# A three-stage kernel whose second products go out two steps at a time at every second step, while the weights are being decoded

## The chip, the core and the metric

The kernel runs on one core of a Trainium2 chip. The metric is the device time of one execution in microseconds (us), the median of several runs. TensorE is called PE here, VectorE DVE, ScalarE ACT, GpSimd POOL, SyncE SP, as in the profile.

## What is computed

A causal convolution over 4 sequences of 4096 tokens with 192 channels, 7 taps and one softmaxed set of taps for each of 8 heads, and then two layers of the form "product, function, product" on the 16384 tokens:

```python
out = np.einsum('hk,bskhg->bshg', w, x_unf)   # w: softmax over the 7 taps
h = x @ w_in                                  # 192 -> 2048
g = h * np.cos(h)
x = g @ w_out                                 # 2048 -> 192
h = x @ w_in2
g = np.where(h > 0.0, h, 1.0 * (np.exp(np.minimum(h, 0.0)) - 1.0))
return g @ w_out2
```

The four weight matrices come as 64-bit floats. The kernel turns each into a pair of 32-bit tiles, a high and a low part, from its two 32-bit words. That is what "decoding" means below.

## The kernel before, in words

**Tiles and steps.** The tokens are 32 blocks of 512. The 2048 hidden channels of a block are done in 8 steps of two tiles of 128. So a step is (layer m, block b, pair j), and there are 512 steps in a list made at lines 509 to 516: four blocks of layer 1, the same four of layer 2, the next four of layer 1, and so on. The first two blocks of layer 1 are each split into two runs of four steps.

**First products (A).** `products_A` makes one hidden tile `u` from x: 9 products of 64 rows each. The two tiles of a step, t = 2s and 2s + 1, use the two halves of PE's rows and stand side by side, 18 products in 9 slots (`side_by_side`, line 577). Each `u` takes the next of four PSUM banks in a ring (lines 518 to 523), so the tiles of step s reuse the banks of step s - 2.

**Elementwise work.** For a tile of layer 1, ACT makes `w` from `u` (line 608, `emit_act1`), DVE subtracts (line 617, `emit_mid`), ACT takes the sine (line 623, `emit_act2`), DVE multiplies by `u` (line 631, `emit_g`; the last reader of the bank), ACT rounds to `gh` (line 637, `emit_hi`), POOL makes `gl` = w - gh (line 644, `emit_lo`). `gh` and `gl` have six buffers each, three steps' worth. Layer 2 has no line 617, and line 633 in the place of line 631.

**Second products (B).** `LAG` = 3 steps later, `gh` and `gl` of a step go into the accumulators. In blocks that begin while weights are still being decoded this is `whole_B`: 10 products over all 128 rows (line 567), placed behind the first products. Two accumulator banks do for it, since the other two PSUM banks hold the decoding's tiles `t`. Once decoding is over (`late`), blocks use `products_B`, 20 products of 64 rows that stand side by side with the first products.

**Order.** The schedule is written out by hand, by the order in which `step` (line 874) emits. It emits all products of step s first, and then for i = 0, 1 and t = 2s + i:

```python
if now:
    emit_act1(t)
    emit_mid(t)
...
if 0 <= t - 1 < 2 * total:
    emit_act2(t - 1)
    emit_g(t - 1)
...
if 0 <= t - 2 < 2 * total:
    emit_hi(t - 2)
    emit_lo(t - 2)
```

Between these stand pieces of the decoding (`advance`: lines 195 to 207 on ACT, DVE and POOL, one piece in most steps, at i = 1), the convolution of later blocks (line 376 on DVE), and the reading out of finished accumulators (`evac`: lines 659, 666, 697). Each engine works its own instructions off in order. The steps with `whole_B` are 0 to 31, layer 1 of the first four blocks; their second products are emitted in steps 3 to 34.

Of the kernel before, what the change touches and what calls it, by code (L numbers as in the profile page):

```python
# [23 lines left out]
LAG = 3  # L24
# [8 lines left out]
def conv_then_two_mlps(ctx, tc, x, weight, w_in1, w_out1, w_in2, w_out2, out):  # L33
# [275 lines left out]
    late = []  # L309
# [3 lines left out]
    def bank(tag, name):  # L313
        pool = ps_u if tag[0] == "u" else ps_a if tag[0] == "a" else late[0]
        return pool.tile([P, N], F32, tag=tag, name=name)
# [181 lines left out]
    def double_z(b):  # L497

        zh, zl, zc = zs.pop(b)
        doubled.add(b)  # L500
        sh, sl, ch, cl = doubles()
        swap(sh, zh)
        swap(sl, zl)
        both_halves(ch, zc[half[0]])
        both_halves(cl, zc[half[1]])
        xs[2, b] = {"oh": zh, "ol": zl, "sh": sh, "sl": sl, "ch": ch, "cl": cl}
        yield

    steps, b0 = [], 0
# [15 lines left out]
    acc, hid, wrk, gs = {}, {}, {}, {}  # L525

    def products_A(t):

        (m, b, j), i = steps[t // 2], t % 2
        x, p = xs[m, b], half[i]  # L530
        u = hid[t] = ring_bank("u")
        ops = [(k, w, h) for k in ("cos" if t > 1 else "ocs") for w, h in (("h", "h"), ("l", "h"), ("h", "l"))]
        for n, (k, w, h) in enumerate(ops):
            at = wi[m, w, "c"][p, j] if k == "c" else wi[m, w, "o"][p, j, i if k == "o" else 1 - i]
            yield u, at, x[k + h][p], n == 0, n == len(ops) - 1

    def products_B(s, i):

        m, b, j = steps[s]
        if (m, b) not in acc:  # L540
            acc[m, b] = [bank(k, "acc") for k in ("a0", "b0", "a1", "b1")]
        o, c, p = acc[m, b][i], acc[m, b][2 + i], half[i]
        h, l, sel = (wo[m, n] for n in ("h", "l", "s"))
        ops = []
        for f in (2 * j, 2 * j + 1):
            gh, gl = gs[f"{s} {f % 2}"]
            st, sp = f == 0, f == NF - 1
            for to, w, g, first, final in ((o, l, gh, st, False), (o, h, gh, False, False), (c, sel, gh, st, False), (o, h, gl, False, sp), (c, sel, gl, False, sp)):
                ops.append((to, w[p, f], g[p], first, final))
        if s == total - 1:  # L550
            ops = [ops[n] for n in (2, 4, 7, 0, 1, 9, 3, 5, 6, 8)]
        yield from ops

    def whole_B(s):

        m, b, j = steps[s]
        begins, stops = (j % (NP // 2) for j in (j, j + 1)) if split_up(m, b) else (j, (j + 1) % NP)
        if not begins:
            acc[m, b] = [bank(k, "acc") for k in ("a0", "a1")]
        o, c = acc[m, b]  # L560
        h, l, sel = (wo[m, n] for n in ("h", "l", "s"))
        (gh0, gl0), (gh1, gl1) = gs[f"{s} 0"], gs[f"{s} 1"]
        f0, f1 = 2 * j, 2 * j + 1
        st, sp = not begins, not stops
        ops = [(o, l, f0, gh0), (o, h, f0, gh0), (c, sel, f0, gh0), (o, l, f1, gh1), (o, h, f1, gh1), (c, sel, f1, gh1), (o, h, f0, gl0), (c, sel, f0, gl0), (o, h, f1, gl1), (c, sel, f1, gl1)]
        for n, (to, w, f, g) in enumerate(ops):
            nc.tensor.matmul(to, lhsT=w[:, f], rhs=g, start=st and n in (0, 2), stop=sp and n >= len(ops) - 2)  # L567

    whole = set()

    def split_up(m, b):
        return m == 1 and b < 2

    def ends_here(m, b, j):
        return j == NP - 1 or split_up(m, b) and j == NP // 2 - 1

    def side_by_side(*streams):

        for pr in zip_longest(*streams):
            for product in pr:  # L580
                if product:
                    o, lhsT, rhs, first, final = product
                    nc.tensor.matmul(o, lhsT=lhsT, rhs=rhs, start=first, stop=final)  # L583

    def products(s):
        now, then = 0 <= s < total, 0 <= s - LAG < total
        if then and steps[s - LAG][2] == 0 and not late:
            whole.add(steps[s - LAG][:2])
        if not then or steps[s - LAG][:2] in whole:
            if now:  # L590
                side_by_side(products_A(2 * s), products_A(2 * s + 1))
            if then:
                whole_B(s - LAG)
        elif not now:
            side_by_side(products_B(s - LAG, 0), products_B(s - LAG, 1))
        else:
            streams = products_B(s - LAG, 0), products_B(s - LAG, 1)
            side_by_side(chain(products_A(2 * s), streams[0]), chain(streams[1], products_A(2 * s + 1)))
        if then:
            for i in (0, 1):  # L600
                del gs[f"{s - LAG} {i}"]

    def emit_act1(s):
        m = steps[s // 2][0]
        u = hid[s]
        w = wk.tile([P, N], F32, tag="w", name="w", bufs=5)
        if m == 1:
            nc.scalar.activation(out=w.bitcast(I32), in_=u, func=AF.Copy, bias=0.25)  # L608
        else:
            nc.scalar.activation(out=w, in_=u, func=AF.Relu, scale=-1.0)  # L610
        wrk[s] = w

    def emit_mid(s):
        m = steps[s // 2][0]
        u, w = hid[s], wrk[s]
        if m == 1:
            nc.vector.scalar_tensor_tensor(out=w, in0=u, scalar=0.25, in1=w.bitcast(I32), op0=ALU.add, op1=ALU.subtract)  # L617

    def emit_act2(s):
        m = steps[s // 2][0]  # L620
        w = wrk[s]
        if m == 1:
            nc.scalar.activation(out=w, in_=w, func=AF.Sin, scale=6.283185)  # L623
        else:
            nc.scalar.activation(out=w, in_=w, func=AF.Exp, scale=-1.0)  # L625
# [9 lines left out]
    def emit_hi(t):  # L635
        gh = wk.tile([P, N], F32R, tag="gh", name="gh", bufs=6)
        nc.scalar.activation(out=gh, in_=wrk[t], func=AF.Copy)  # L637
        gs[f"{t // 2} {t % 2}"] = [gh]
# [8 lines left out]
    def evac(m, b, j):  # L647

        if split_up(m, b):
            return first_part(m, b) if j < NP - 1 else second_part(m, b)  # L650
        if (m, b) in whole:
            return whole_evac(m, b)
        return half_evac(m, b)
# [184 lines left out]
    def need(m, at, *kinds):  # L838
        while any(ready.get((k, m), 0) < at for k in kinds):
            assert loaded or any(stages.values())  # L840
            advance()
# [13 lines left out]
    def begin_split(b):  # L855
        while b not in conved:
            next(cq, None)
        for _ in split(b):
            yield
# [14 lines left out]
    def step(s):  # L874
        now = 0 <= s < total
        present[0] = s
        if now:
            m, b, j = steps[s]
            need(m, j + 1, "o", "c")
        finish = iter(())  # L880
        if 0 <= s - LAG < total:
            m, b, j = steps[s - LAG]
            need(m, 2 * j + 2, "oh", "os")
        products(s)
        ends = 0 <= s - LAG < total and ends_here(*steps[s - LAG])
        if ends:
            assert not lazy
            finish = evac(*steps[s - LAG])
        if s in begin_at:
            m, b = begin_at[s]  # L890
            chores.append(begin_split(b) if m == 1 else double_z(b))
        first_mlp = now and steps[s][0] == 1
        for i in (0, 1):
            t = 2 * s + i
            if i:
                next(finish, None)
# [3 lines that stand above are left out]
            next(finish, None)  # L900
# [3 lines that stand above are left out]
            if not prepared and (s < NP // 2 or i != ends and (s < 12 or not ends and (s % 3 or s > 18))):  # L904
                advance()
# [3 lines that stand above are left out]
            if i:  # L909
                next(finish, None)  # L910
            if now and not first_mlp and not ends:
                next(cq, None)
                if i and not first_mlp and steps[s][2] in (4, 6):
                    next(cq, None)
            chore()
        if prepared and not late:
            brief.close()
            top.close()
            late.append(ctx.enter_context(tc.tile_pool(name="ps_s", bufs=1, space=bass.MemoryType.PSUM)))

    total = len(steps)
# [119 lines left out]
```

## Time and profile before

| | |
|---|---|
| Median of 3 runs | 2296.68 us (2296.4 to 2298.99) |
| Profiled execution: its own time / its span | 2297.01 / 2295.3 us |
| PE, DVE, ACT, POOL busy, share of the span | 99%, 77%, 81%, 55% |
| Chain that ended last: PE / DVE | 89% / 8% |
| Granted TensorE clock, mean | 0.997 |
| Line 567, products of the whole form | 47 to 222 us, 32 steps |

All stages bar the first tenth look alike: PE has no gap, and two kinds of product share its rows. The change concerns the stretch from 45 to 222 us alone, so the page's shares of the whole span say little about it. It is read from the order in time of PE's products in that stretch, from what ended the gaps between them, and from what DVE and ACT did meanwhile. A row of the order in time gives the start in us, the duration in us, the engine, the line and the operation, and in a bracket the idle time ahead of it and what ended that.

### The profile page before, as it was taken

Reading aid. Unit: us, or ns where it says so; the run is one execution under the profiler, and the core shown is the slowest. Engines: PE = TensorE matmul, PEld = TensorE weight load, DVE = VectorE, ACT = ScalarE, POOL = GpSimd, SP = SyncE. Lnnn points to the kernel's source line nnn. Section 1 sums busy time; section 2 is a strip of 40 time slices with the busy share of each in tenths; the row PEclk is TensorE's granted clock in tenths of the full one; section 3 lists DMA queues with packets and bytes.
Section 4 is the critical chain, followed back from the end, with each engine's and each line's share of the span. In section 5 each row is a group of like instructions: output and inputs, shape, how many; then the busy total and the mean of one; then the engine's idle time right before and its main releaser. Section 6 shows DMA issues by size and latency. Waiting matters only on the chain.

```text
span 2295.3 us, 49382 instructions
## 1 busy us (share of the span) xinstructions
PE 2265.7 (99%) x19226; PEld 1839.5 (80%) x19226; DVE 1768.8 (77%) x2564; ACT 1862.8 (81%) x3422; POOL 1253.0 (55%) x975
## 2 busy tenths in 40 slices
PE   8999999999999999999999999999999999999998
PEld 5667888888888888888888888888888888888887
DVE  7986977779777897778967798676986779777655
ACT  6877788888888788888788888888788887888886
POOL 5895335763367533674446743576435763367532
PEclk9999999999999999999999999999999999999999
DMA  7222221213211132112221123212221113211111
GB/s 167 81 68 49 51 58 36 46 32 64 49 36 38 32 69 48 40 29 57 52 52 33 24 58 55 47 38 44 45 57 35 46 34 64 42 36 38 26 38 22
DMA packets 292603, 111.43 MB, mean 49 GB/s; under 512 B 245840, under 2 KB 260176, under 8 KB 292368
## 3 DMA queue, kind: packets, MB, share of 16 engines
q1 hardware_dynamic: 290048, 107.42, 22.4%
q8 instruction: 150, 2.46, 0.4%
q10 hardware_dynamic: 2320, 0.85, 0.2%
q14 instruction: 85, 0.70, 0.1%
HBM read 30.09 MB, written 12.58 MB: 19 GB/s over the span
## 4 chain that ended last, share of the span: by engine, by line
PE 89%; DVE 8%; issue 1%; ACT 1%; DMA 1%; POOL 0%; ACTq 0%; DVEq 0%; SPq 0%; POOLq 0%
PE acc L583 45%; PE u L583 42%; DVE y L376 1%; PE acc L567 1%; DVE w L633 1%; DVE w L631 1%; DVE w L617 1%; DVE gl L644 1%; DVE t L202 1%; DVE w L203 0%; DMA raw<-in_moe_w_in_dram 0%; DMA raw<-in_moe_w_out_dram 0%; DVE y L374 0%; DVE raw L199 0%; PE y L403 0%
## 5 line engine op out<-in xcount | busy, mean ns | idle before, releaser
L644 POOL TENSOR_TENSOR gl<-w,gh 128x512 fp32r<-128x512 f32 x768 | 1013.7, 1321 | 1001.8 <-ACT gh L637 640.0
L583 PE MATMUL acc<-gh,wo_hl 64*128 64x512 f32 x3840 | 1174.3, 386 | 0.0
L583 PEld LDWEIGHTS acc<-gh,wo_hl 64*128 64x128 f32 x3840 | 705.3, 184 | 75.8 <-DVE z L697 0.4
L583 PE MATMUL acc<-gh,wo_s 64*128 64x512 f32 x1920 | 740.8, 386 | 0.0
L583 PE MATMUL acc<-gl,wo_hl 64*128 64x512 f32 x1920 | 740.2, 386 | 0.0
L583 PE MATMUL acc<-gl,wo_s 64*128 64x512 f32 x1920 | 740.1, 386 | 0.0
L637 ACT ACTIVATE gh<-w 128x512 fp32r<-128x512 f32 x1024 | 641.2, 626 | 16.2 <-DVE w L633 15.8
L583 PE MATMUL u<-ch,wi_c 64*128 64x512 f32 x2048 | 619.4, 391 | 14.1 <-DVE w L631 11.4
L583 PE MATMUL u<-sh,wi_o 64*128 64x512 f32 x2048 | 611.4, 387 | 0.0
L617 DVE SCALAR_TENSOR_TENSOR w<-u,w 128x512 f32<-128x512 f32 x512 | 352.0, 687 | 251.1 <-ACT w L608 249.1
L633 DVE SCALAR_TENSOR_TENSOR w<-w,u 128x512 f32<-128x512 f32 x512 | 347.8, 679 | 215.1 <-ACT w L625 210.0
L610 ACT ACTIVATE w<-u 128x512 f32<-128x512 f32 x512 | 306.2, 598 | 186.7 <-PE u L583 167.1
L608 ACT ACTIVATE w<-u 128x512 int32<-128x512 f32 x512 | 306.4, 598 | 184.2 <-PE u L583 178.5
L583 PE MATMUL u<-z,wi_o 64*128 64x512 f32 x1536 | 427.4, 386 | 0.0
L583 PEld LDWEIGHTS u<-ch,wi_c 64*128 64x128 f32 x2048 | 364.7, 184 | 71.7 <-DVE w L631 18.9
L583 PEld LDWEIGHTS u<-sh,wi_o 64*128 64x128 f32 x2048 | 368.5, 185 | 40.7
L583 PE MATMUL u<-sl,wi_o 64*128 64x512 f32 x1024 | 387.1, 387 | 0.0
L583 PE MATMUL u<-cl,wi_c 64*128 64x512 f32 x1024 | 386.7, 387 | 0.0
L583 PEld LDWEIGHTS acc<-gh,wo_s 64*128 64x128 f32 x1920 | 353.3, 184 | 37.9 <-DVE e L698 0.3
L583 PEld LDWEIGHTS acc<-gl,wo_hl 64*128 64x128 f32 x1920 | 353.3, 184 | 37.6
L583 PEld LDWEIGHTS acc<-gl,wo_s 64*128 64x128 f32 x1920 | 353.2, 184 | 37.6
L631 DVE TENSOR_TENSOR w<-u,w 128x512 f32<-128x512 f32 x512 | 348.8, 681 | 41.4 <-ACT w L623 41.4
(143 smaller groups left out, 3608.2 us busy)
## 6 DMA issues: line engine op xcount, KB each, us to landing
out_dram<-e SPq DMA_DIRECT2D x189, 64.0 KB, 2.0
xa<-in_x_dram SPq DMA_DIRECT2D x124, 88.0 KB, 2.9
sh<-z SPq DMA_DIRECT2D x64, 128.0 KB, 2.9
sl<-z SPq DMA_DIRECT2D x64, 128.0 KB, 2.5
ch<-z SPq DMA_DIRECT2D x64, 128.0 KB, 2.4
cl<-z SPq DMA_DIRECT2D x64, 128.0 KB, 2.4
sh<-xh SPq DMA_DIRECT2D x62, 128.0 KB, 2.3
sl<-xl SPq DMA_DIRECT2D x62, 128.0 KB, 2.3
```

The source lines that it names most:

```text
L202: nc.vector.tensor_scalar(out=t, in0=size, scalar1=2.0 ** -15, scalar2=2.0 ** 17 - 2.0 ** 13, op0=ALU.max, op1=ALU.min)
L376: nc.vector.scalar_tensor_tensor(out=o, in0=i, scalar=w, in1=o, op0=ALU.mult, op1=ALU.add)
L567: nc.tensor.matmul(to, lhsT=w[:, f], rhs=g, start=st and n in (0, 2), stop=sp and n >= len(ops) - 2)
L583: nc.tensor.matmul(o, lhsT=lhsT, rhs=rhs, start=first, stop=final)
L608: nc.scalar.activation(out=w.bitcast(I32), in_=u, func=AF.Copy, bias=0.25)
L610: nc.scalar.activation(out=w, in_=u, func=AF.Relu, scale=-1.0)
L617: nc.vector.scalar_tensor_tensor(out=w, in0=u, scalar=0.25, in1=w.bitcast(I32), op0=ALU.add, op1=ALU.subtract)
L631: nc.vector.tensor_tensor(out=w, in0=u, in1=w, op=ALU.mult)
L633: nc.vector.scalar_tensor_tensor(out=w, in0=w, scalar=-1.0, in1=u, op0=ALU.add, op1=ALU.max)
L637: nc.scalar.activation(out=gh, in_=wrk[t], func=AF.Copy)
L644: eng.tensor_tensor(out=gl, in0=wrk.pop(t), in1=f32(own[0]), op=ALU.subtract)
```

## The change

At even steps the second products of the two steps s - 4 and s - 3 are emitted together, behind the first products of step s. At odd steps there are none. This holds for blocks in the whole form; blocks of the other form are as before. Nothing is computed differently, and no buffer is added.

```diff
-    def products(s):
-        now, then = 0 <= s < total, 0 <= s - LAG < total
-        if then and steps[s - LAG][2] == 0 and not late:
-            whole.add(steps[s - LAG][:2])
-        if not then or steps[s - LAG][:2] in whole:
+    def is_whole(s):
+        if steps[s][2] == 0 and not late:
+            whole.add(steps[s][:2])
+        return steps[s][:2] in whole
+
+    def due(s):
+        if not 0 <= s - LAG < total:
+            return []
+        if not is_whole(s - LAG):
+            return [s - LAG]
+        return [s - LAG - 1, s - LAG] if (s - LAG) % 2 else []
+
+    def products(s, then):
+        now = 0 <= s < total
+        if not then or is_whole(then[0]):
             if now:
                 side_by_side(products_A(2 * s), products_A(2 * s + 1))
-            if then:
-                whole_B(s - LAG)
+            for k in then:
+                whole_B(k)
...
-        if 0 <= s - LAG < total:
-            m, b, j = steps[s - LAG]
+        then = due(s)
+        for k in then:
+            m, b, j = steps[k]
             need(m, 2 * j + 2, "oh", "os")
-        products(s)
-        ends = 0 <= s - LAG < total and ends_here(*steps[s - LAG])
+        products(s, then)
+        ends = bool(then) and ends_here(*steps[s - LAG])
```

The order on PE, before, around one step of the whole form: from the last first products of one step to the start of the next step's. `u` is a hidden tile, `acc` an accumulator; 128x512 is the output.

```order
L583 MATMUL u<-sl,wi_o 128x512 x2
L567 MATMUL acc<-gh,wo_hl 128x512 [waits Pool_49]
L567 MATMUL acc<-gh,wo_hl 128x512 [waits Activation_49]
L567 MATMUL acc<-gh,wo_s 128x512
L567 MATMUL acc<-gh,wo_hl 128x512 x2
L567 MATMUL acc<-gh,wo_s 128x512
L567 MATMUL acc<-gl,wo_hl 128x512
L567 MATMUL acc<-gl,wo_s 128x512
L567 MATMUL acc<-gl,wo_hl 128x512
L567 MATMUL acc<-gl,wo_s 128x512
L583 MATMUL u<-ch,wi_c 128x512 [waits DVE_49] x2
```

On PE after the change, from the last first products of an odd step, through all first products of the even step behind it, to the first second product:

```order
L583 MATMUL u<-sl,wi_o 128x512 x2
L583 MATMUL u<-ch,wi_c 128x512 [waits DVE_49] x2
L583 MATMUL u<-ch,wi_c 128x512 x2
L583 MATMUL u<-cl,wi_c 128x512 x2
L583 MATMUL u<-xh,wi_o 128x512 x4
L583 MATMUL u<-xl,wi_o 128x512 x2
L583 MATMUL u<-sh,wi_o 128x512 x4
L583 MATMUL u<-sl,wi_o 128x512 x2
L567 MATMUL acc<-gh,wo_hl 128x512 [waits Pool_49]
```

What moved: the ten second products that stood between two steps' first products are gone from behind the odd step, and stand as a second ten behind the even step's.

On DVE the order is the same before and after. This is the change's, with the tiles' numbers (u_834 and u_835 are step 8's, u_907 and u_908 step 9's, u_956 step 10's; lines 628 and 642 are lines 617 and 631 of before):

```order
L628 SCALAR_TENSOR_TENSOR w_927<-u_907,w_927 128x512 [waits Activation_49]
L642 TENSOR_TENSOR w_885<-u_835,w_885 128x512 [waits Activation_49]
L628 SCALAR_TENSOR_TENSOR w_936<-u_908,w_936 128x512 [waits Activation_49]
L642 TENSOR_TENSOR w_927<-u_907,w_927 128x512 [waits Activation_49]
L199 SCALAR_TENSOR_TENSOR raw_173<-raw_173,t_95 128x512 [waits DMAHW7_49,DMAHW0_49]
L202 TENSOR_SCALAR t_95<-w_897 128x512 [waits DVE_49]
L203 TENSOR_SCALAR w_897<-t_95 128x512 [waits DVE_49]
```

Nothing moved here: the last reading of step 8's second bank (u_835) stands behind the first instruction that needs step 9's first products (u_907). What moved is PE's side of it.

On ACT the order of the work is the same too, and a wait is another. Before, in step 8:

```order
L637 ACTIVATE gh_881<-w_815 128x512 [waits DVE_49]
L608 ACTIVATE w_885<-u_847 128x512 [waits PE_49,Pool_49]
L623 ACTIVATE w_876<-w_876 128x512 [waits DVE_49]
L254 ACTIVATE wo1_hl_475<-w_709 128x512 [waits Pool_49]
L195 ACTIVATE t_95<-raw_173 128x512 [waits DMAHW7_49,DMAHW0_49]
```

After:

```order
L648 ACTIVATE gh_881<-w_803 128x512 [waits DVE_49,PE_49]
L619 ACTIVATE w_885<-u_835 128x512 [waits Pool_49]
L634 ACTIVATE w_876<-w_876 128x512 [waits DVE_49]
L254 ACTIVATE wo1_hl_475<-w_699 128x512 [waits Pool_49]
L195 ACTIVATE t_95<-raw_173 128x512 [waits DMAHW7_49,DMAHW0_49]
```

What moved is the wait on PE, from the reading of `u` to the writing of `gh`: that buffer's last reader now stands on PE behind the same step's first products. POOL's and SP's instructions stand as before.

## Rows read from the trace of the kernel before

**Rows 1.** The chain that ended last, from the page: shares of the span.
```profile
PE 89%; DVE 8%; issue 1%; ACT 1%; DMA 1%; POOL 0%; ACTq 0%; DVEq 0%; SPq 0%; POOLq 0%
```

**Rows 2.** Busy time by stretch (PE, PEld, DVE, ACT, POOL), then clock, DMA share, GB/s.
```profile
44.90:221.50 176.60, 164.31 (x897) 114.30 (x896) 146.94 (x214) 139.88 (x260) 141.63 (x109) 0.98 0.32 80
221.50:398.10 176.60, 176.60 (x1555) 145.46 (x1556) 141.53 (x202) 144.89 (x267) 74.39 (x56) 1.00 0.23 46
```

**Rows 3.** Order in time on PE, one step without gaps: start, duration, instruction.
```profile
192.79 0.73 PE L583 MATMUL u<-ch,wi_c 64*128 64x512 f32 x4
...
194.74 0.39 PE L583 MATMUL u<-sl,wi_o 64*128 64x512 f32 x2
195.06 0.73 PE L567 MATMUL acc<-gh,wo_hl 128*128 128x512 f32 x2
...
195.86 0.62 PE L567 MATMUL acc<-gh,wo_hl 128*128 128x512 f32 x2
...
197.25 0.40 PE L567 MATMUL acc<-gl,wo_s 128*128 128x512 f32 x1
197.58 0.50 PE L583 MATMUL u<-ch,wi_c 64*128 64x512 f32 x2
```

**Rows 4.** Order in time on ACT and DVE behind those first products.
```profile
195.22 0.60 ACT L608 ACTIVATE w<-u 128x512 int32<-128x512 f32 x1 [1.32 <-PE u L583]
195.72 0.62 ACT L623 ACTIVATE w<-w 128x512 f32<-128x512 f32 x1
...
196.46 0.68 DVE L631 TENSOR_TENSOR w<-u,w 128x512 f32<-128x512 f32 x1
```

**Rows 5.** DVE's last reading of a bank, and the product on PE that waited for it.
```profile
101.70 0.68 DVE L631 TENSOR_TENSOR w<-u,w 128x512 f32<-128x512 f32 x1
...
102.44 0.74 PE L583 MATMUL u<-ch,wi_c 64*128 64x512 f32 x3 [0.56 <-DVE w L631]
```

**Rows 6.** PE's waits from 44 to 222 us: total, times, longest.
```profile
PE u L583 <- DVE w L631: 11.4, 13, 1.8
```

**Rows 7.** Order in time on PE: four long waits, and the next step's start behind two.
```profile
56.75 0.73 PE L583 MATMUL u<-ch,wi_c 64*128 64x512 f32 x3 [1.77 <-DVE w L631]
...
63.07 0.73 PE L583 MATMUL u<-ch,wi_c 64*128 64x512 f32 x4
...
114.12 0.73 PE L583 MATMUL u<-ch,wi_c 64*128 64x512 f32 x3 [1.62 <-DVE w L631]
...
136.10 0.80 PE L583 MATMUL u<-ch,wi_c 64*128 64x512 f32 x3 [1.52 <-DVE w L631]
...
142.44 0.73 PE L583 MATMUL u<-ch,wi_c 64*128 64x512 f32 x4
...
160.80 0.73 PE L583 MATMUL u<-ch,wi_c 64*128 64x512 f32 x3 [1.69 <-DVE w L631]
```

**Rows 8.** PE by stretch behind three of these waits; the last-but-two column is the clock.
```profile
57.90:61.20 3.30, 3.30 (x15) 0.53 0.44 110
...
115.90:119.20 3.30, 3.15 (x17) 1.00 0.86 152
...
136.40:139.70 3.30, 3.30 (x17) 0.53 0.02 5
```

**Rows 9.** Order in time on DVE: first line 617 of steps 3, 5, 7, 9, 17, 19.
```profile
48.04 0.69 DVE L617 SCALAR_TENSOR_TENSOR w<-u,w 128x512 f32<-128x512 f32 x1 [3.57 <-ACT w L608]
...
60.14 0.69 DVE L617 SCALAR_TENSOR_TENSOR w<-u,w 128x512 f32<-128x512 f32 x1 [0.19 <-ACT w L608]
...
72.16 0.68 DVE L617 SCALAR_TENSOR_TENSOR w<-u,w 128x512 f32<-128x512 f32 x1
...
84.28 0.68 DVE L617 SCALAR_TENSOR_TENSOR w<-u,w 128x512 f32<-128x512 f32 x1
...
127.77 0.68 DVE L617 SCALAR_TENSOR_TENSOR w<-u,w 128x512 f32<-128x512 f32 x1
...
140.20 0.69 DVE L617 SCALAR_TENSOR_TENSOR w<-u,w 128x512 f32<-128x512 f32 x1
```

More of the change, by code (lines that the diff above doesn't have):

```diff
@@ L583, in side_by_side @@
                     nc.tensor.matmul(o, lhsT=lhsT, rhs=rhs, start=first, stop=final)
-    def products(s):
-        now, then = 0 <= s < total, 0 <= s - LAG < total
-        if then and steps[s - LAG][2] == 0 and not late:
-            whole.add(steps[s - LAG][:2])
-        if not then or steps[s - LAG][:2] in whole:
+    def is_whole(s):
[11 more added lines that the diff above has]
+        if not then or is_whole(then[0]):
             if now:
                 side_by_side(products_A(2 * s), products_A(2 * s + 1))
-            if then:
-                whole_B(s - LAG)
+            for k in then:
+                whole_B(k)
         elif not now:
-            side_by_side(products_B(s - LAG, 0), products_B(s - LAG, 1))
+            side_by_side(products_B(then[0], 0), products_B(then[0], 1))
         else:
-            streams = products_B(s - LAG, 0), products_B(s - LAG, 1)
+            streams = products_B(then[0], 0), products_B(then[0], 1)
             side_by_side(chain(products_A(2 * s), streams[0]), chain(streams[1], products_A(2 * s + 1)))
-        if then:
+        for k in then:
             for i in (0, 1):
-                del gs[f"{s - LAG} {i}"]
+                del gs[f"{k} {i}"]
     def emit_act1(s):
@@ L880, in step @@
         finish = iter(())
-        if 0 <= s - LAG < total:
-            m, b, j = steps[s - LAG]
+        then = due(s)
+        for k in then:
+            m, b, j = steps[k]
             need(m, 2 * j + 2, "oh", "os")
-        products(s)
-        ends = 0 <= s - LAG < total and ends_here(*steps[s - LAG])
+        products(s, then)
+        ends = bool(then) and ends_here(*steps[s - LAG])
         if ends:
```

## The prediction, made before the changed kernel was run

> **What bounds the kernel now.** I read the chain of the page first: PE is 89% of it, one line of products after another [rows 1]. So time is won or lost where PE is held up, or where its own products get cheaper. Then I split the busy times by stretch. In the 176.6 us from the first product of step 3 to that of step 35, the stretch that the change touches, PE works 164.3 us; in the next 176.6 us it works all of them [rows 2]. So PE has 12.3 us of gaps in the changed stretch and none behind it, and whatever that stretch gains or loses is handed on whole to the end. In the changed stretch DVE is at 147 of 176.6 us [rows 2], so it is near to being a second limit.
>
> Then the order in time on PE, in a step without a gap [rows 3]. It takes 197.58 - 192.79 = 4.79 us: 2.27 us from the first A product to the first B product, 2.52 us from there to the next step's A. Within B six products go out in 197.25 - 195.86 = 1.39 us, so a slot is 0.232 us. The step has 9 + 10 = 19 slots, 4.40 us. The other 0.39 us lie at the two changes between A (two products of 64 rows side by side) and B (128 rows).
>
> Then who waits for whom. Of the 12.3 us of gaps 11.4 us are one kind of wait, 13 times: a first product waits for DVE's last reading of its bank [rows 6]. So the ring of four banks is what couples PE to DVE, and the change alters just what stands between two users of a bank.
>
> **What is saved.** With two B together, each pair of steps has one change from A to B and one back, where it had two of each. There are 16 pairs, so 16 x 0.39 = 6.2 us less on PE [rows 3].
>
> **What is added.** The two tiles of step s reuse the banks of step s - 2. The last reading of the second of them is the line 631 of tile 2(s - 2) + 1. On DVE it stands behind the line 617 of step s - 1's first tile, on ACT its sine stands behind that tile's line 608, and both of these need step s - 1's A to be complete. So from the end of one step's A to the second product of the next step's A there is always a chain through ACT and DVE. Its length, from a step in which neither engine had a backlog: A's last products start at 194.74 and take 0.39, so they end at 195.13 [rows 3]; line 608 starts at 195.22, line 623 at 195.72, line 631 at 196.46 for 0.68, so it ends at 197.14 [rows 4]. That is 2.01 us. From there to the released product it is 0.06 us: 101.70 + 0.68 = 102.38, against 102.44 [rows 5].
>
> Before, B's 2.52 us lie over this chain, so it shows only where DVE is late. After the change nothing lies between an odd step's A and the even step's A. The cover is gone there, 16 times, and it is useless where two B follow one another: behind the even step's A PE has 2 x 10 slots to do.
>
> So a pair costs PE, where nothing else is late: A of the even step to B 2.27, ten slots and the change back 2.52, another ten slots 2.32, the odd step's A 2.34 to its end (192.79 to 195.13), the chain 2.01 and 0.06. Sum 11.52 us, against 2 x 4.79 = 9.58 us. The sum over the stretch: step 3's A and its chain 2.34 + 2.07 = 4.41; fifteen pairs at 11.52 = 172.8; the last even step with its two B 2.27 + 2.52 + 2.32 = 7.11. That is 184.3 us, against 176.6 us [rows 2]: **+7.7 us**. The 6.2 us saved are in it, and so are the old waits, which go, as DVE now has 11.52 us for what it did in 11.0 on average.
>
> **Where DVE is slower than that.** Some pairs have more than 11.52 us of DVE work. From the first line 617 of one odd step to that of the next it was: steps 3 and 4 60.14 - 48.04 = 12.10, less the idle 0.19 in the second row's bracket, 11.91; 5 and 6 12.02; 7 and 8 12.12; 17 and 18 12.43 [rows 9]. The excess over 11.52 is 0.4 + 0.5 + 0.6 + 0.9 = 2.4 us at most, as DVE may still have been idle for some tenths inside the others; I take **+2.0 us**. I found no other pair with more than 11.52 us of work.
>
> **What the clock adds.** Four old waits are about as long as the new one. Behind 56.75 and 136.10 the granted clock fell to the lower of its two levels, 1.2 GHz (0.53 on average over 3.3 us, so 0.5 for nearly all of it); behind 114.12 it stayed at 1.00 [rows 7, 8], and so it did behind 160.80. The two falls cost 63.07 - 56.75 = 6.32 and 142.44 - 136.10 = 6.34 us for a step that takes 4.79 [rows 3, 7], so 1.54 us each. The new wait, shown as such a row shows it (behind the lone first product, which starts one slot after A's last and takes 0.50), would be idle for about 2.46 - 0.23 - 0.50 = 1.73 us. The nearest rows are 1.77, which fell, and 1.69, which did not; 1.62 did not and 1.52 did [rows 7]. The bounds are none and all 16. I take 10: a little over the half that the four show, since 1.73 is at the long end of them. That is 10 x 1.54 = 15.4 us, less what the pairs limited by DVE absorb, 2.0 x 10/16 = 1.3: **+14.1 us**.
>
> The Trainium skill (TensorE: Matmul & The Clock Gate, section Why this matters for your kernels) warns only of idle gaps longer than any wait here. By that the clock would not fall at all, and the sum would be 2306.4. The trace disagrees: it fell behind idle times of 1.77 and 1.52 us [rows 7, 8].
>
> **What I cost at nothing.** `gh` of an even step's first tile now waits for the third product of the first B. In the step of the rows that product would start a slot before 195.86, at 195.63, and be out some 0.4 us later, at 196.03; ACT first does lines 608 and 623, until 195.72 + 0.62 = 196.34 [rows 3, 4]. Its second `gh` and POOL's `gl` wait for products that are out before their engines get there. The cover is the two B, 4.8 us in which ACT and POOL have only that step to do; if it failed, 0.3 us a pair, 5 us in all, would be the price. The decoding is placed by step and not by time, so DVE, ACT, POOL and SP do the same in the same order, DMAs too. Reading out a finished accumulator gets a step more of room; the 0.9 us of PE's gaps that are not line 631's [rows 2, 6] go, inside the sum above.
>
> **The sum.** 2297.0 us (the profiled execution) + 7.7 + 2.0 + 14.1 = 2320.8. The median of the runs is 0.3 us lower, so 2320.5 us.
>
> **Rivals.**
> 1. *The wait comes, the clock hardly falls.* 2297.0 + 9.7 - 0.3 = 2306.4 us with no fall, 1.5 us more for each of a few. For it: two of the four long waits left the clock alone. Against it: sixteen waits of one length come one behind the other, and some must lie as those that fell.
> 2. *Faster.* The new wait takes the place of the old ones, which are there already for 11.4 us [rows 6], and the saved changes remain: 2296.7 - 6.2 = 2290.5 us. This decides at one point: the last reading of the second bank would have to end within a slot of the odd step's last A product. For it: where DVE has a backlog, it has the next tile's input before PE asks. Against it: by the order on DVE that reading stands behind an instruction that needs those very products, so 2.0 us are the least, and where DVE has no backlog it takes 2.01 us [rows 3, 4].
> 3. *No difference.* The saved changes and the freed backlog of DVE pay for the new wait, about 2297 us. This needs the chain at 1.5 us instead of 2.07; no row shows it so short.
> 4. *Slower still.* All waits pull the clock down, and `gh` costs its 0.3 us a pair: 2297.0 + 9.7 + 16 x 1.54 - 2.0 + 5 = 2334 us.
> That the change doesn't do what it says is excluded: PE's order shows 16 pairs.
>
> **Chances.** The forecast, with five to fourteen falls: 0.58. Rival 1: 0.25. Rival 2: 0.08. Rival 3: 0.04. Rival 4: 0.05. Differences under 0.2% (4.6 us) are about what a measurement of this kernel can't tell from none. So faster 0.08, same 0.04, slower 0.88. The range: rival 1 without any fall, and 2 us for the error of a chain taken from one step (16 x 0.13), give 2304; fourteen falls, 14 x 1.54 = 21.6, less 1 that DVE's pairs absorb, plus the same 2, give 2329. Rivals 2 to 4 are left out, 0.17 in all.
>
> **What would show it.** In the changed kernel, line 567's products in groups of twenty; 16 waits of a first product for DVE's line of `g`, each 1.5 to 1.8 us as the rows count, some 27 us in all in the place of 11.4; a granted clock of about 0.9 instead of 0.98 in the stretch, with 0.5 for 3 us behind many of the waits; the first split products at 240 to 248 us instead of 221.5; and everything behind that as before, only later. The prediction is wrong if those waits are few or short, if the clock stays at 1.00, or if the time comes from behind 250 us.

## The result, and the profile after

| | before | after |
|---|---|---|
| Median | 2297.3 us | 2323.8 us |
| Lowest to highest | 2296.4 to 2298.99 | 2323.12 to 2327.97 |
| Profiled execution: time / span | 2297.01 / 2295.3 us | 2323.89 / 2322.2 us |
| Mean granted clock | 0.997 | 0.990 |

The ratio is 1.0118, with a 95% interval of 1.0101 to 1.0136. The kernel became slower by 26.5 us, where 23.8 us were forecast.

The busy times by stretch of the kernel after, columns as in [rows 2]. The first line runs from the first product of step 3 to that of step 35, the same pieces of work as the first of [rows 2]:

```profile
45.50:248.80 203.30, 170.31 (x899) 124.31 (x898) 151.04 (x216) 141.80 (x262) 140.24 (x109) 0.91 0.28 69
248.80:425.40 176.60, 176.60 (x1559) 145.95 (x1560) 141.46 (x200) 144.44 (x266) 73.95 (x55) 1.00 0.24 46
```

The stretch takes 203.3 us where it took 176.6. That is 26.7 us, the whole loss; behind it PE works all the time again, as before. PE's gaps went from 12.3 to 33.0 us, and its busy time from 164.3 to 170.3 us though it has the same products to do: the clock is 0.91 instead of 0.98.

PE's waits in the stretch, total, times and longest, are the counterpart of [rows 6] (line 642 is line 631 of before, line 644 its like in layer 2):

```profile
PE u L583 <- DVE w L642: 31.2, 15, 3.5
PE u L583 <- DVE w L644: 1.8, 1, 1.8
```

There are sixteen of them, one for each pair, and together they are all of PE's 33.0 us of gaps. The order in time on PE, one pair in which the clock stayed up and the start of the next:

```profile
204.30 0.73 PE L583 MATMUL u<-ch,wi_c 64*128 64x512 f32 x3 [1.95 <-DVE w L642]
...
211.35 0.73 PE L583 MATMUL u<-ch,wi_c 64*128 64x512 f32 x4
...
213.31 0.40 PE L583 MATMUL u<-sl,wi_o 64*128 64x512 f32 x2
213.54 0.39 PE L583 MATMUL u<-ch,wi_c 64*128 64x512 f32 x1
215.77 0.77 PE L583 MATMUL u<-ch,wi_c 64*128 64x512 f32 x3 [1.83 <-DVE w L642]
...
228.74 0.73 PE L583 MATMUL u<-ch,wi_c 64*128 64x512 f32 x3 [1.83 <-DVE w L642]
```

And what ACT and DVE did between 213.31 and 215.77:

```profile
213.79 0.60 ACT L619 ACTIVATE w<-u 128x512 int32<-128x512 f32 x1 [3.53 <-PE u L583]
214.29 0.62 ACT L634 ACTIVATE w<-w 128x512 f32<-128x512 f32 x1
...
215.03 0.68 DVE L642 TENSOR_TENSOR w<-u,w 128x512 f32<-128x512 f32 x1
```

The odd step's A ends at 213.31 + 0.40 = 213.71. DVE's last reading ends at 215.71, 2.00 us later, and the released product starts at 215.77. From one such release to the next it is 215.77 - 204.30 = 11.47 us here, and 228.74 - 215.77 = 12.97 us in the next pair. The difference is the clock, by stretch (PE busy, clock, DMA share, GB/s):

```profile
216.30:219.70 3.40, 3.40 (x16) 0.50 0.00 0
...
204.40:207.70 3.30, 3.30 (x22) 1.00 0.02 5
```

Behind the release at 204.30 PE started 22 products in 3.3 us; behind the one at 215.77 it started 16 in 3.4 us, at 1.2 instead of 2.4 GHz. Ten of the sixteen waits are followed by such a fall, nine times of about 3.4 us and once, behind 138.93, of 6.8.

### The profile page after: what moved, and what is told of

Read it like the earlier page. It is cut to its first block, busy times and chain, and to the rows that moved or that the text cites. A ratio compares the mean times of both kernels' runs of the same rounds, so it can differ in the third digit from the quotient of the medians.

```text
span 2322.2 us, 49396 instructions
## 1 busy us (share of the span) xinstructions
PE 2270.5 (98%) x19226; PEld 1862.8 (80%) x19226; DVE 1772.8 (76%) x2564; ACT 1862.6 (80%) x3422; POOL 1250.5 (54%) x975
## 4 chain that ended last, share of the span: by engine, by line
PE 91%; DVE 6%; issue 1%; ACT 1%; DMA 0%; ACTq 0%; POOL 0%; DVEq 0%; POOLq 0%
PE acc L583 45%; PE u L583 43%; PE acc L567 3%; DVE y L376 1%; DVE w L644 1%; DVE gl L655 1%; DVE w L642 1%; DVE w L628 1%; DVE t L202 0%; DVE y L374 0%; ACT w L619 0%; DMA raw<-in_moe_w_in_dram 0%; PE y L403 0%; DVE raw L199 0%; DVE w L203 0%
```

## The experiments

Theory: the new wait is the chain from the odd step's A through ACT and DVE to the last reading of the second bank; it is 2 us long, comes 16 times, and the clock falls behind most of them. Rivals: twenty second products in a row cost something by themselves, for instance through `gh` and `gl`, which come free later; only the clock counts, or does not count at all; the loss belongs to the decoding.

**The chain taken away.** In the changed kernel, at the start of odd steps, the instructions of the tile before go first:

```diff
+            early = i == 0 and 3 <= s < 34 and s % 2 == 1
+            if early:
+                emit_act2(t - 1)
+                emit_g(t - 1)
             if now:
                 emit_act1(t)
                 emit_mid(t)
             next(finish, None)
-            if 0 <= t - 1 < 2 * total:
+            if not early and 0 <= t - 1 < 2 * total:
                 emit_act2(t - 1)
                 emit_g(t - 1)
```

> The change, with the sine and the product by u of the tile before (lines 623 and 631 of before) emitted ahead of lines 608 and 617 at the start of each odd step from 3 to 33. My theory (the new wait is the chain from the odd step's first products through ACT and DVE to the last reading of the second bank): that reading no longer needs the odd step's products, the 16 waits go, the clock stays up, and the 16 x 0.39 us of saved changes remain where DVE is not the limit: 2290 to 2297 us. Rival (twenty second products in a row cost by themselves, through gh and gl that come free later): about 2315 to 2324, as the changed kernel. Rival (only the clock counts): waits stay at 1.8 us, 2305 to 2324.

Measured: 2301.33 us against 2298.96 us before, ratio 1.0009 (0.9999 to 1.0018). Some 24 of the 26.5 us are gone, with the second products still in twenties. That speaks for the chain and against the rivals that put the cost on the twenties themselves. The size expected was not met: the time should have come out under before. PE's waits of this run, and two starts of odd steps' A in a part without any wait:

```profile
PE u L583 <- DVE w L642: 18.2, 14, 2.5
...
197.19 0.73 PE L583 MATMUL u<-ch,wi_c 64*128 64x512 f32 x4
...
206.30 0.73 PE L583 MATMUL u<-ch,wi_c 64*128 64x512 f32 x4
```

Where nothing waits, a pair takes 206.30 - 197.19 = 9.11 us, where it took 9.58 before [rows 3]. So the saving on PE is real, 0.47 us a pair. But 18.2 us of other waits are left, more than the 11.4 us of before, and the clock of the stretch is 0.95, from five falls. One of these waits on DVE, ending with line 642 at 141.53:

```profile
138.92 1.27 DVE L677 SCALAR_TENSOR_TENSOR rows<-acc,rows 128x512 f32<-128x512 f32 x2
140.12 0.73 DVE L376 SCALAR_TENSOR_TENSOR y<-xT,wch,y 128x512 f32<-128x512 f32 x1
141.53 0.69 DVE L642 TENSOR_TENSOR w<-u,w 128x512 f32<-128x512 f32 x1 [0.68 <-ACT w L634]
```

The reading out of an accumulator (line 677) and a convolution tap (line 376) stand ahead of the reading that PE waits for, and ACT's sine for it stands behind a reading that needs line 677. With two A in a row PE asks for that bank right away; with ten B in between it asked 2.5 us later [rows 3]. The other thirteen waits were not followed up in this way.

**The control.** The same reordering in the kernel before, without the change.

> The same reordering in the kernel before, as a control. My theory: before, the second products lie over the chain, and the 11.4 us of waits there come from DVE's work for the decoding; putting one 0.6 us instruction later changes little: 2292 to 2298 us. If the reordering is worth more than 5 us by itself, what the run before this one gains is not the change's.

Measured: 2297.15 us against 2298.96 us, ratio 0.9997 (0.9988 to 1.0006). No difference, as expected. So what the reordering won in the changed kernel it won by taking the new wait away, and not by something of its own.

**The wait kept, PE kept busy.** In the changed kernel, eight copies of a first product in front of the even step's A:

```diff
+                a, c = products_A(2 * s), products_A(2 * s + 1)
+                if then:
+                    head = next(a)
+                    for _ in range(8):
+                        nc.tensor.matmul(head[0], lhsT=head[1], rhs=head[2], start=True, stop=True)
+                    a = chain([head], a)
-                side_by_side(products_A(2 * s), products_A(2 * s + 1))
+                side_by_side(a, c)
```

> The change, with eight copies of the even step's first product (64 rows, into the same free bank, overwritten by the real one) in front of it, so that PE works for about 1.85 of the 2.0 us of the wait. The result is the same. My theory of the clock (it falls behind these waits, 11 times in the trace, for 1.5 us each): the waits' place in time stays, no fall, 2323.8 - 11 x 1.5 = 2307 us (2304 to 2311). Rival (the falls cost nothing, since DVE or ACT set the pace): 2320 or more.

Measured: 2309.27 us against 2298.96 us, ratio 1.0046 (1.0032 to 1.0060). That is 14.5 us under the changed kernel by the medians and, as 1.0118 - 1.0046 = 0.0072, 16.5 us by the ratios, though PE has 128 products more to do. It lies inside the range expected. (The text ahead of the run counts the long fall as two.) The stretch by halves, columns as in [rows 2], and the copies with what stands around them:

```profile
45.24:145.00 99.76, 97.58 (x546) 72.30 (x547) 88.38 (x129) 78.83 (x148) 78.79 (x61) 1.00 0.35 84
145.00:232.00 87.00, 85.94 (x475) 64.22 (x472) 58.75 (x85) 61.68 (x115) 61.92 (x49) 0.98 0.26 65
```
```profile
199.70 0.73 PE L583 MATMUL u<-ch,wi_c 64*128 64x512 f32 x4
...
201.89 1.98 PE L606 MATMUL u<-ch,wi_c 64*128 64x512 f32 x8
203.71 1.14 PE L583 MATMUL u<-ch,wi_c 64*128 64x512 f32 x4
...
211.16 0.73 PE L583 MATMUL u<-ch,wi_c 64*128 64x512 f32 x4
```

The copies fill the wait, the pair takes 211.16 - 199.70 = 11.46 us as a pair without a fall does in the changed kernel, and one fall is left where there were ten. So the falls are a cost of their own: nine of them are worth some 14 to 17 us. The 10 to 12 us that are left come from the waits, with the one fall.

**Half of the cover given back.** In the changed kernel the first five of the ten products of the earlier step stay behind the odd step's A:

```diff
...
+            for k in ahead:
+                whole_B(k, 0, HEAD)
             for k in then:
-                whole_B(k)
+                whole_B(k, HEAD * (k == then[0]))
...
```

`ahead` is `[s - LAG]` at odd steps and empty at even ones, and `HEAD` is 5: `whole_B(k, lo, hi)` emits the products from `lo` to `hi` - 1.

> The change, with the first five of the ten products of the earlier step put back behind the odd step's first products. My theory: they cover 1.2 to 1.5 of the 2.07 us of the chain, the waits shrink to about 0.5 us, the clock stays up, a pair takes 10.4 us on PE, and DVE's share of the old waits comes back: 2299 to 2305 us. Rival (what costs is that the second products come in lumps and late): it keeps most of the loss, 2312 or more.

Measured: 2301.44 us against 2298.96 us, ratio 1.0010 (1.0001 to 1.0019), within what the theory expected. In a part where DVE is light:

```profile
194.88 0.73 PE L583 MATMUL u<-ch,wi_c 64*128 64x512 f32 x4
...
198.52 0.50 PE L583 MATMUL u<-ch,wi_c 64*128 64x512 f32 x1
199.30 0.73 PE L583 MATMUL u<-ch,wi_c 64*128 64x512 f32 x3 [0.27 <-DVE w L644]
...
205.21 0.73 PE L583 MATMUL u<-ch,wi_c 64*128 64x512 f32 x4
```

The wait shrinks from 1.83 to 0.27 us and a pair takes 205.21 - 194.88 = 10.33 us, where 10.4 were expected. (Line 644 is line 631 of before here.) Five products are 1.16 us, and the pair became 11.47 - 10.33 = 1.14 us shorter. Over the whole stretch 14.0 us of waits for DVE are left, and the clock is 0.99.

**The last block alone.** The change for steps 24 to 31 alone:

```diff
-        if not is_whole(s - LAG):
+        if not is_whole(s - LAG) or steps[s - LAG][:2] != (1, 3):
```

> The change for the last of the four blocks alone (steps 24 to 31, whose second products go out in steps 27 to 34), where little decoding is left; the three blocks before it are as in the kernel before. Four pairs, four new waits. My theory (each pair 11.5 instead of 9.6 us, and two in three falls of the clock at 1.5 us): 4 x 1.9 + 3 x 1.5 = 12 us more than before, 2307 to 2313 us. Rival (the loss comes with the decoding, since DVE and POOL are full there): within 4 us of before.

Measured: 2309.92 us against 2298.05 us, ratio 1.0047 (1.0032 to 1.0063): 11.9 us for four pairs, where 12 were expected. The rival that ties the loss to the decoding is out, as there is little of it left in these steps.

> The run before this one, with lines 623 and 631 of the tile before emitted first in the odd steps 27 to 33. With the change on all blocks this took the waits away in the last pairs (9.11 us a pair) and left 18 us of other waits in the decoding. My theory (those others are DVE's lumps of decoding, met by two steps' first products in a row, and pairs pay only where DVE is light): four pairs at 0.4 to 0.5 us, so 1.5 to 2 us under before, 2294 to 2297.5 us. Rival (the order of lines 623 and 631 costs something of its own): at or over before.

Its edit is the one line above and the reordering at the top, for steps 27 to 33. Measured: 2300.51 us against 2298.05 us, ratio 1.0006 (0.9997 to 1.0015). This missed: the time is not under before. Two of the four pairs take 9.11 and 9.10 us, but the first one met a wait of 2.06 us and a fall of the clock. On ACT ahead of that wait's end, the reading out of the block before (lines 706, 707 and 715) stands in front of the sine:

```profile
185.29 0.58 ACT L706 ACTIVATE z<-acc 128x512 fp32r<-128x512 f32 x1
185.89 0.60 ACT L707 ACTIVATE e<-acc 64x512 f32<-64x512 f32 x1
187.24 0.63 ACT L715 ACTIVATE z<-e 64x512 fp32r<-64x512 f32 x1 [0.75 <-DVE e L709]
187.77 0.61 ACT L634 ACTIVATE w<-w 128x512 f32<-128x512 f32 x1
```

So decoding is not the only lump that two A in a row run into; the theory's "lumps of decoding" have to be read as anything that stands in front of the bank's last reader.

**All steps reordered.** `early` at every step from 3 to 34, odd and even.

> The change with lines 623 and 631 of the tile before emitted first in every step from 3 to 34, odd and even. Theory (the waits left in the run with odd steps alone are DVE's lumps of decoding): they stay within a few us, 2296 to 2303 us. Rival (they come from the even steps' own chain): the 18 us of waits fall under 8, and the time to 2290 to 2294 us.

Measured: 2301.79 us against 2298.05 us, ratio 1.0013 (1.0004 to 1.0022). This lies in the theory's range, and the rival's 2290 to 2294 us were not reached. The profile, of the slowest of the ten runs (2307.32 us), has 21.6 us of waits for line 642 and not under 8. So the even steps' own chain was not what held up the run with odd steps.

**Both together.** The chain taken away at odd steps, and four copies in front of A at even steps up to 26.

> The run with lines 623 and 631 emitted first in odd steps, and four copies of the even step's first product in front of it in the even steps up to 26 (about 0.9 us of PE's work, overwritten by the real product, so the result is the same). In that run 18.2 us of waits and five falls of the clock were left in the stretch. My theory (those waits are set by DVE and ACT and not by PE, so PE's extra work lies inside them, and the falls are most of what it lost): 2301.3 - 5 x 1.5 = 2294 us with no fall, 2294 to 2299 us. Rival (the waits that are left set the time by themselves, and the falls lie inside them): 2300 to 2306 us.

Measured: 2298.26 us against 2299.0 us, ratio 0.9995 (0.9986 to 1.0004). This lies in the range expected, at its upper end: by the ratios the run gained some 3 us on the one with odd steps alone, give or take 3, where five falls at 1.5 us would be 7.5. The clock stays up through the whole stretch (columns as in [rows 2]):

```profile
44.90:223.00 178.10, 165.84 (x949) 123.12 (x947) 145.71 (x216) 140.57 (x261) 142.11 (x109) 1.00 0.32 79
```

Part of what is missing stands in PE's rows: its waits for DVE, and the starts of two odd steps' A, with an even step and its copies in between.

```profile
PE u L583 <- DVE w L648: 10.3, 12, 1.6
PE u L606 <- DVE w L648: 0.9, 2, 0.5
...
103.26 0.73 PE L583 MATMUL u<-ch,wi_c 64*128 64x512 f32 x4
...
113.25 0.50 PE L583 MATMUL u<-ch,wi_c 64*128 64x512 f32 x1
```

Some 11 us of waits are left, two of them in front of the copies. And where no wait comes, the copies cost: this pair takes 113.25 - 103.26 = 9.99 us instead of 9.11, and so do two others, 2.6 us in all. So without falls and without the new chain the changed order, with these copies, is as fast as before and no faster. Whether it would be faster with copies only where a wait comes was not tried. No version here beats the kernel before by more than the comparison can tell.

## Why the prediction was right, point by point

**What bounds the kernel.** Right: the loss arose in the one stretch and was handed on whole, 26.7 us there and 26.5 us in the medians.

**What is saved.** Right in kind, 0.47 us a pair against 0.39, seen only where neither wait nor lump stands in the way.

**The chain.** Right in kind, place and length: 2.00 us against 2.01, 0.06 us to the release, 11.47 us a pair against 11.52, sixteen times. The run without it gave back some 24 us, the run with half of the cover took 1.1 us off a pair. The waits as the rows show them were a little longer than the 1.5 to 1.8 us forecast: 1.82 us at the least, 3.53 at the most, and 33.0 us in all against 27.

**DVE's excess.** Right in kind, too small in size. These are some of the rows in which DVE's last reading released PE, from the start of the stretch and from its middle:

```profile
49.98 0.73 PE L583 MATMUL u<-ch,wi_c 64*128 64x512 f32 x3 [1.91 <-DVE w L642]
...
61.80 0.72 PE L583 MATMUL u<-ch,wi_c 64*128 64x512 f32 x3 [2.10 <-DVE w L642]
...
74.81 0.73 PE L583 MATMUL u<-ch,wi_c 64*128 64x512 f32 x3 [1.83 <-DVE w L642]
...
86.95 1.22 PE L583 MATMUL u<-ch,wi_c 64*128 64x512 f32 x3 [2.51 <-DVE w L642]
...
125.77 0.73 PE L583 MATMUL u<-ch,wi_c 64*128 64x512 f32 x3 [1.83 <-DVE w L642]
...
138.93 1.22 PE L583 MATMUL u<-ch,wi_c 64*128 64x512 f32 x3 [3.53 <-DVE w L642]
...
153.01 0.74 PE L583 MATMUL u<-ch,wi_c 64*128 64x512 f32 x3 [1.89 <-DVE w L642]
...
165.24 1.22 PE L583 MATMUL u<-ch,wi_c 64*128 64x512 f32 x3 [2.60 <-DVE w L642]
```

Of the five pairs without a fall one took 11.47 us from release to release, the others 11.82, 12.14, 13.16 and 12.23: 3.5 us over, where 2.0 were forecast. The two of them that the prediction lists came out as listed: 11.82 us from 49.98 on against 11.91, and 12.14 from 74.81 on against 12.12. The other two are pairs in which it found no such work. In the pair from 125.77 on, 1.7 us over, DVE spent 3.60 us on one convolution tap (the last section), which no row of before could have shown. The pair from 153.01 on, 0.8 us over, could have been seen. DVE took 152.50 - 140.20 = 12.30 us for it before [rows 9]. That is under 11.52 only without the 0.83 us in which DVE waited for ACT. The wait came again, and the 12.30 us with it: 163.91 - 151.61. First before, then after:

```profile
142.38 0.69 DVE L617 SCALAR_TENSOR_TENSOR w<-u,w 128x512 f32<-128x512 f32 x1 [0.83 <-ACT w L608]
...
152.50 0.68 DVE L617 SCALAR_TENSOR_TENSOR w<-u,w 128x512 f32<-128x512 f32 x1
```
```profile
151.61 0.69 DVE L628 SCALAR_TENSOR_TENSOR w<-u,w 128x512 f32<-128x512 f32 x1 [1.24 <-ACT w L619]
153.79 0.69 DVE L628 SCALAR_TENSOR_TENSOR w<-u,w 128x512 f32<-128x512 f32 x1 [0.83 <-ACT w L619]
...
163.91 0.68 DVE L628 SCALAR_TENSOR_TENSOR w<-u,w 128x512 f32<-128x512 f32 x1
```

So idle time of DVE inside a chain that runs through ACT is not room that a longer pair fills.

**The clock.** Right in kind, and in number by luck in part: ten falls were put down from four old waits, behind two of which the clock had fallen, and ten came. The length of the wait does not tell them apart, as the clock fell behind waits of 1.83 us (215.77) and stayed up behind others of 1.83 (74.81, 125.77). In size it was too small. By all sixteen releases, the ten pairs with a fall took 130.95 us together, 16.3 us over ten times 11.47, where 14.1 were forecast. One fall was twice as long, and its pair, from 138.93 on, took 14.08 us; the other nine took 12.85 to 13.11. A fall alone cost 12.97 - 11.47 = 1.50 us, against 1.54. DVE's excess did not come on top of a fall: the pair from 61.80 on, with 12.02 us of DVE's work by the prediction, took 13.01 us, and the one from 215.77 on, with little, 12.97. That is the absorbing that the prediction reckoned with.

**The sum.** Step 3's A and chain, fifteen pairs at 11.47 and the tail come to 183.6 us; with 3.5 and 16.3 us that is the 203.3 us measured, within a tenth. The forecast was 184.3, 2.0 and 14.1. Between the +23.8 us forecast and the stretch's +26.7 lie 2.9 us: 1.5 and 2.2 us from the two terms that were too small, less 0.7 from the shorter pair.

The Trainium skill (TensorE: Matmul & The Clock Gate, section Why this matters for your kernels) warns of idle gaps that are longer than fifteen of these sixteen waits. That shorter ones do no harm does not follow here: the clock fell behind nine of the fifteen, the shortest of 1.83 us.

**What was costed at nothing.** `gh` waited for PE six times, 3.1 us in all, and POOL's `gl` 14.7 us; neither shows up among PE's waits, so a cost of nothing is right for the path. But the prediction had no such waits at all, and here they were.

**The rivals.** The clock did fall, so the first is out. The second, faster, is out by the order on DVE, as argued; and with the chain removed by hand it still did not come out: other waits for DVE, 18.2 us, and five falls took the saving.

## What to carry to other kernels

Products that stand between two uses of a buffer ring are cover, whatever else they are: before grouping them, name the chain that frees the buffer and its length, and look for what is left to lie over it on each side of the group. Here a group saved 0.4 us and uncovered 2.0 us. And a short wait on TensorE that comes back again and again can cost nearly as much again through its clock: here 1.5 us on top of 2.0, behind ten waits of sixteen.

## What the runs showed of the hardware that was not expected

One convolution tap on DVE, with the same shape as the others, took 3.60 us, where the shortest of the stretch took 0.74; in the same time POOL ran two-operand instructions without a gap:

```profile
134.08 3.60 DVE L376 SCALAR_TENSOR_TENSOR y<-xT,wch,y 128x512 f32<-128x512 f32 x1
137.60 0.68 DVE L628 SCALAR_TENSOR_TENSOR w<-u,w 128x512 f32<-128x512 f32 x1
138.20 0.67 DVE L642 TENSOR_TENSOR w<-u,w 128x512 f32<-128x512 f32 x1
```
```profile
134.62 1.27 POOL L234 TENSOR_TENSOR wi_o<-w,wi_o 128x512 fp32r<-128x512 f32 x1
135.86 2.94 POOL L655 TENSOR_TENSOR gl<-w,gh 128x512 fp32r<-128x512 f32 x2
```

In the kernel before the longest was 1.93 us. The two readings of the chain stand right behind it, and PE's longest wait, 3.53 us, ended at 138.93, 0.06 us after the second of them.

The trace points at POOL as the cause. Of the fourteen taps of the stretch three took 0.74 us, two of them with POOL idle beside them. Ten others took 1.12 to 1.85 us, and each of these ended 0.54 to 0.61 us after a POOL instruction beside it ended. In the two rows that follow, for example, POOL ends at 242.79 and the tap at 243.33:

```profile
241.50 1.29 POOL L655 TENSOR_TENSOR gl<-w,gh 128x512 fp32r<-128x512 f32 x1 [2.98 <-ACT gh L648]
...
241.61 1.72 DVE L376 SCALAR_TENSOR_TENSOR y<-xT,wch,y 128x512 f32<-128x512 f32 x1
```

The tap of 3.60 us would then have waited through several POOL instructions. But the profile's spans on POOL are rough, and no run took POOL's instructions away, so the cause is not shown.
